# Gathering expert 3's rows earlier, and turning one row tile of expert 2 on TensorE, in an attention kernel followed by a hash-routed mixture of experts

## The chip, the cores and the metric

The kernel runs on one core of one Trainium2 chip. The metric is the device time of one execution in microseconds (us); lower is better. A core has TensorE (PE in the profile; its weight loads stand apart as PEld), VectorE (DVE), ScalarE (ACT), GpSimd (POOL) and SyncE (SP). 16 DMA engines move data between memory in HBM and the core's SBUF.

## The reference

The first half is attention over 8 batches, 12 heads, 448 positions and a head size of 64, with normalised q and k. Its output, as 3584 rows of 768 values, goes to the second half, in which each row is sent to one of 8 experts by a hash of its token id:

```
expert_idx = token_ids * 2654435761 % E          # E = 8
for e in range(E):
    mask = expert_idx == e
    xe = x[mask]                                  # about 448 rows of 768
    h = np.maximum(xe @ w1[e], 0.0)               # w1[e]: 768 x 1024
    out[mask] = h @ w2[e]                         # w2[e]: 1024 x 768
```

The change lies in the second half alone.

## The kernel before

**Attention** fills the first 160 us or so. It writes its rows, in fp16, to a scratch tensor in HBM (`x_scratch`), and a table of row numbers by expert (`gidx`) is worked out beside it.

**The experts** follow one after the other, e = 0 to 7. Each has 480 slots for its rows: three row tiles of 128 and one of 96 (`KT` = 4, `LAST` = 96). An expert goes through these steps.

- *Gather* (`fetch`, line 230): four indirect DMAs issued by POOL bring its rows from `x_scratch` into a ring of eight row tiles, `xg_ring` (the tile is called kr in the profile). Experts with an even number use tiles 0 to 3 of the ring, those with an odd number tiles 4 to 7.
- *Turn*: the rows must be turned, so that the 768 input values lie across the partitions, into `xT` (two buffers, used in turn by the experts). For experts 2 to 6 VectorE does it, in 16 instructions of 32 partitions each that take all four row tiles at a time (`turn_blocks`, line 1072). Experts 0 and 1 are turned by TensorE, six transposes for a row tile (`turn`, which calls `put_xT`: line 242, with a copy out of PSUM in line 244). Expert 7 is turned by four DMA transposes on SP.
- *First product* (`gemm1`, line 1002, 48 matmuls), whose result ScalarE evicts into `h_sb` (line 1011). It reads all of `xT` from its first matmul on.
- *Second product* (`gemm2`, line 1024, 16 matmuls for each of the four row tiles), evicted into `o_sb` (line 1034), from which POOL issues one indirect DMA for each row tile, the scatter, into the output (line 1037).

**Weights** come from HBM in five pieces an expert (three of w1, two of w2), each a DMA that POOL issues (`w_next`, line 1105) and that casts from fp32 to fp16. They are listed in `queue` and issued at fixed places in the program: two after an expert's first product, one behind each row tile of the second product, and what is left at the expert's end.

So POOL's program is one list of gathers, scatters and weight loads, all on one DMA queue. Each of these DMAs belongs to one of eight semaphores in turn, and the issue of a DMA waits for the one eight places before it, which had the same semaphore.

The order of work comes from the order in which the code is written (there is no scheduler). Two tables add work at given places: `plan[e, "k", kt]` lists functions that are called behind row tile kt of expert e's second product, and `before[e, kt]` functions that are called ahead of it. In the loop over the experts the places that the change touches are these:

```
            if e < E - 2:
                fetch(e + 2, range(KT))
                turn_blocks(e + 1)
            gemm1(...)
        if e:
            w_next(2)
```

Expert 2 is fetched in `plan[0, "k", 2]`, and expert 3 at the top of e = 1 by the lines above, behind the `w_next(len(queue))` that ends e = 0.

Of the kernel before, what the change touches and what calls it, by code (L numbers as in the profile page):

```python
# [20 lines left out]
def kernel(  # L21
# [30 lines left out]
    LAST = FIT - 3 * P  # L52
    KT = CAP // P
# [175 lines left out]
    def gather(xg, idx, rows=N):  # L229
        nc.gpsimd.indirect_dma_start(  # L230
            out=xg[0:idx.shape[0], :], out_offset=None, in_=x_dram[0:rows, :],
            in_offset=bass.IndirectOffsetOnAxis(ap=idx, axis=0),
            bounds_check=rows - 1, oob_is_err=False)
        return xg
# [729 lines left out]
    with tc.manual_schedule(), \  # L964
# [10 lines left out]
        def w1_view(e, w1_sb):  # L975
            return w1_sb[:].rearrange("p c (o f) -> p c o f" if e == 0 else "p c (f o) -> p c o f",
                                      o=FO)
# [13 lines left out]
        def gemm1(w1v, xT, h_sb, c0, c1, both=True, after=(), apart=0):  # L991
            banks = {}

            def products(fo, a0, a1):
                if fo not in banks:
                    banks[fo] = ps_h.tile([P, 512], FP32, name="h_ps")
                dst = banks[fo][:, a0 - c0:a1 - c0]
                if xT is xT_e:
                    dst = dst.rearrange("p (k t) -> p k t", t=P)
                for co in range(CO):  # L1000
                    src = xT[:, a0 // P:a1 // P, co, :] if xT is xT_e else xT[:, co, a0:a1]
                    nc.tensor.matmul(dst, lhsT=w1v[:, co, fo, :], rhs=src,  # L1002
                                     start=(co == 0), stop=(co == CO - 1))

            for fo in range(apart):
                products(fo, c0, c1 - P)
            for fo in range(FO):
                products(fo, c1 - P if fo < apart else c0, c1)
                h_ps = banks.pop(fo)
                if fo % 2 == 0 or not both:  # L1010
                    nc.scalar.activation(h_sb[:, fo, c0:c1], h_ps[:, :c1 - c0], AF.Relu)  # L1011
                else:
                    nc.vector.tensor_scalar(out=h_sb[:, fo, c0:c1], in0=h_ps[:, :c1 - c0],
                                            scalar1=0.0, scalar2=None, op0=ALU.max)
                for f in after[fo] if after else ():
                    f()

        def gemm2(w2_sb, h_sb, col, idx, free=True, between=None, last=False, by_v=True):
            w = LAST if free and col == KT - 1 else P
            o_ps = [ps_o.tile([P, DIN], FP32, name="o_ps")]  # L1020
            o_ps.append(ps_o.tile([P, DIN], FP32, name="o_ps") if last else o_ps[0])
            for d0, d1 in ((0, 512), (512, DIN)):
                for fo in range(FO):
                    nc.tensor.matmul(o_ps[d0 > 0][0:w, d0:d1], lhsT=h_sb[:, fo, col * P:col * P + w],  # L1024
                                     rhs=w2_sb[:, fo, d0:d1],
                                     start=(fo == 0), stop=(fo == FO - 1))
                if between and d0 == 0:
                    between()
                if last and d0 == 0:
                    o_sb = m_o.tile([P, DIN], FP32, name="o_sb")  # L1030
                    nc.scalar.copy(o_sb[0:w, 0:512], o_ps[0][0:w, 0:512])
            if not last:
                o_sb = m_o.tile([P, DIN], FP32, name="o_sb")
                (nc.vector.tensor_copy if by_v and col % 2 else nc.scalar.copy)(o_sb[0:w], o_ps[0][0:w])  # L1034
            else:
                nc.scalar.copy(o_sb[0:w, 512:DIN], o_ps[1][0:w, 512:DIN])
            scat = nc.gpsimd.indirect_dma_start(  # L1037
                out=out[:, :], out_offset=bass.IndirectOffsetOnAxis(ap=idx[0:w], axis=0),
                in_=o_sb[0:w], in_offset=None, bounds_check=N - 1, oob_is_err=False)
            if free:  # L1040

                tc.declare_no_dep(scat.ins, group="scatters", reason="disjoint rows")
                tc.add_to_no_dep_group("scatters", scat.ins)
# [4 lines left out]
        def fetch(e, kts):  # L1048
            for kt in kts:
                c = e * KT + kt  # L1050
                xgs[c] = gather(xg_ring[:, c % (2 * KT)],
                                gidx[0:P if kt < KT - 1 else LAST, c:c + 1],
                                N_EARLY if kt < KT - 1 else N)

        def turn(e, kt, copy=None):
            if e not in xTs:
                xTs[e] = m_x.tile([P, CO, CAP], FP16, name="xT")
            bank = ps_x.tile([P, DIN], FP16, name="xT_ps")
            put_xT(xgs.pop(e * KT + kt), xTs[e], kt, bank[:], copy)

        def turn_blocks(e):
            xT = xTs[e] = m_x.tile([P, CO, CAP], FP16, name="xT")
            c0 = e * KT % (2 * KT)
            xg = xg_ring[:, c0:c0 + KT].rearrange("p k (c m r) -> p k m c r", m=4, r=32)
            dst = xT[:].rearrange("p c (g r) -> p c g r", r=32)
            for kt in range(KT):
                xgs.pop(e * KT + kt)
            for i in range(4):
                n = KT if 32 * i < LAST else KT - 1
                g = slice(i, i + 4 * (n - 1) + 1, 4)  # L1070
                for m in range(4):
                    nc.vector.transpose(  # L1072
                        out=dst[32 * m:32 * m + 32, :, g].rearrange("p c k r -> p k c r"),
                        in_=xg[32 * i:32 * i + 32, 0:n, m])

        def turn_by_dma(e):
            xTs[e] = m_x.tile([P, CO, CAP], FP16, name="xT")
            for kt in range(KT):
                n = P if kt < KT - 1 else LAST
                nc.sync.dma_start_transpose(out=xTs[e][:, :, kt * P:kt * P + n],  # L1080
                                            in_=xgs.pop(e * KT + kt)[0:n, :])
# [20 lines left out]
        def w_next(n):  # L1102
            for _ in range(min(n, len(queue))):
                o, i = queue.pop(0)
                nc.gpsimd.dma_start(out=o, in_=i)  # L1105
# [135 lines left out]
        def each(f, *parts):  # L1241
            return [lambda p=p: f(p) for p in parts]
# [3 lines left out]
            (0, "g", 4): [p7, p8], (0, "g", 5): [p9, p10, p11],  # L1246
            (0, "g", 6): each(low, 0, 1), (0, "g", 7): each(low, 2, 3), (0, "k", 0): [high],
            (0, "k", 1): [high_tok], (0, "k", 2): [table_mm, lambda: fetch(2, range(KT))],
            (1, "k", 0): [overflow_table],
        }  # L1250
        t = lambda e, kt: (lambda: turn(e, kt))
        t0 = lambda e, kt: (lambda: turn(e, kt, nc.scalar.copy))
        before, between = {}, {}
# [2 lines left out]
        before[0, 2] = [lambda: gemm1_late(w1_view(0, w_tiles[0][0]), xTs.pop(0), hs[0], EARLY, FIT)]  # L1256
        between[0, 2] = t0(1, 2)
        before[0, 3] = [t(1, 3)]
        hs = {}
        fetch(0, [KT - 1])  # L1260
        fetch(1, [KT - 1])
# [2 lines left out]
        for e in range(E):  # L1264
            w1_sb, w2_sb = w_tiles[e]
            h_sb = hs[e] = m_h.tile([P, FO, CAP], FP16, name="h_sb")
            after = [plan.get((e, "g", fo), []) for fo in range(FO)]
            if e == 0:
                gemm1(w1_view(e, w1_sb), xTs[e], h_sb, 0, EARLY, False, after, 2)
            else:  # L1270
                if e == E - 2:
                    turn_by_dma(E - 1)
                if e < E - 2:
                    fetch(e + 2, range(KT))
                    turn_blocks(e + 1)
                gemm1(w1_view(e, w1_sb), xTs.pop(e), h_sb, 0, FIT, e >= E - 2, after)
            if e:
                w_next(2)
            if e == 2:
                n_ov = nc.values_load(novi[0:1, 0:1], min_val=0, max_val=NOV)  # L1280
            if e == E - 1:
                nc.gpsimd.drain()
            for kt in range(KT):
                c = e * KT + kt
                for f in before.get((e, kt), []):
                    f()
                gemm2(w2_sb, h_sb, kt, gidx[:, c:c + 1], between=between.get((e, kt)),
                      last=(c == E * KT - 1), by_v=e in (0, E - 2, E - 1))
                for f in plan.get((e, "k", kt), []):
                    f()  # L1290
                if e or kt > 1:
                    w_next(1)
            w_next(len(queue))
            if e + 4 < E:
                queue += w_pieces(e + 4)
# [47 lines left out]
```

## Time and profile before

| what | value |
|---|---|
| time, median of 3 runs | 333.07 us (332.08 to 333.38) |
| time of the profiled execution | 332.74 us |
| span of the profiled execution, first to last instruction | 331.1 us |
| TensorE busy (matmuls) | 318.2 us, 96% of the span |
| VectorE busy | 239.3 us, 72% |
| ScalarE busy | 207.5 us, 63% |
| GpSimd busy | 149.5 us, 45% |
| GpSimd's DMA queue (q0) | 58.32 MB; its packets took 87.7% of 16 engines' span |
| granted TensorE clock, mean | 0.994 |

A time is the device time of a whole execution; the span leaves out 1.6 us around the first and last instruction of the profiled one. TensorE is busy nearly all the time, but matmuls are pipelined and their ends are modelled, so that a row of matmuls can end after the next one starts. The start times are the ones to go by.

### The profile page before, as it was taken

To read this page: it belongs to the slowest core of one execution; us is meant where nothing else is said; L and a number is where in the kernel's file an instruction comes from. 1 tells how busy PE (TensorE), PEld (TensorE's weight loads), DVE (VectorE), ACT (ScalarE), POOL (GpSimd) and SP (SyncE) were. 2 spreads that over 40 slices of the span, in tenths; PEclk is the share of its full clock that TensorE was granted. 3 is DMA by queue.
4 is the path that set the end of the run, shared out by engine and by line. 5 is a ranking of instruction groups with operands and counts; after the bars stand their busy time and mean duration, and the time that the engine had idled before them with its cause. 6 is when DMAs were issued, how large, how long until landed. Compare 5 with 4: busy or idle time off the path is not lost. (4 is left out here: it accounts for less than half of the span.)

```text
span 331.1 us, 8985 instructions
## 1 busy us (share of the span) xinstructions
PE 318.2 (96%) x3765; PEld 219.7 (66%) x3765; DVE 239.3 (72%) x457; ACT 207.5 (63%) x317; POOL 149.5 (45%) x207
## 2 busy tenths in 40 slices
PE   7699999999999999999999999999999999999992
PEld 3467777777777777666767766666676675766761
DVE  4689999898999999985694397693958939422210
ACT  4699999999999999999543333424334253321211
POOL 8799944432441100003475872655727556403122
PEclk9999999999999999999999999999999999999997
DMA  6999999999999999722478699999999999993013
GB/s 122 197 202 203 194 242 196 236 200 240 203 240 212 245 225 227 164 70 70 124 152 211 165 207 242 244 264 265 265 272 239 254 253 260 307 174 137 23 48 124
DMA packets 45601, 65.52 MB, mean 198 GB/s; under 512 B 12727, under 2 KB 33423, under 8 KB 45432
## 3 DMA queue, kind: packets, MB, share of 16 engines
q0 software_dynamic: 39072, 58.32, 87.7%
q1 hardware_dynamic: 6328, 6.50, 7.5%
q8 instruction: 30, 0.49, 0.6%
q10 hardware_dynamic: 160, 0.11, 0.1%
q14 instruction: 11, 0.09, 0.1%
HBM read 89.29 MB, written 17.30 MB: 322 GB/s over the span
## 5 line engine op out<-in xcount | busy, mean ns | idle before, releaser
L660 ACT ACTIVATE expT<-sc_ps 128x896 bf16<-128x896 f32 x144 | 125.1, 960 | 1.0 <-PE sc_ps L637 0.7
L1072 DVE STREAM_TRANSPOSE xT<-kr 32x768 f16<-32x768 f16 (+1 forms) x80 | 73.6, 920 | 25.7 <-DMA kr<-x_scratch,gidx 15.2
L1024 PEld LDWEIGHTS <-h_sb 128*128 128x128 f16 (+1 forms) x512 | 52.2, 104 | 31.3
L1024 PE MATMUL o_ps<-w_sb,h_sb 128*128 128x512 f16 (+3 forms) x384 | 64.2, 326 | 0.0
L1011 ACT ACTIVATE h_sb<-h_ps 128x480 f16<-128x480 f32 (+1 forms) x56 | 31.3, 560 | 48.6 <-PE h_ps L1002 48.6
L1037 POOL DMA_INDIRECT out_dram<-o_sb,gidx x32 | 35.1, 1097 | 57.6 <-ACT o_sb L1034 29.6
L1034 ACT COPY o_sb<-o_ps 128x768 f32<-128x768 f32 (+1 forms) x26 | 20.8, 799 | 54.5 <-PE o_ps L1024 54.5
L230 POOL DMA_INDIRECT kr<-x_scratch,gidx x32 | 32.6, 1020 | 49.3 <-DVE qT L629 37.1
L1002 PEld LDWEIGHTS <-w_sb 128*128 128x128 f16 x300 | 39.8, 135 | 16.4 <-issue 0.7
L1002 PE MATMUL h_ps<-xT,w_sb 128*128 128x480 f16 x240 | 49.4, 366 | 0.3 <-DVE xT L1072 0.3
L637 PE MATMUL sc_ps<-qT,kT 64*128 64x448 f16 x288 | 44.4, 356 | 0.5 <-DVE qT L629 0.4
L678 PEld LDWEIGHTS <-expT 128*128 128x128 bf16 x846 | 36.8, 97 | 9.2 <-DVE x_sb L738 4.4
L678 PE MATMUL av_ps<-v,expT 128*128 128x65 bf16 x828 | 41.5, 193 | 0.1
L306 POOL DMA_DIRECT2D vr<-in_v_dram x36 | 23.7, 670 | 20.8 <-DMA kr<-in_k_dram 11.5
L738 DVE TENSOR_TENSOR x_sb<-av_ps,srec 128x448 f16<-128x448 f32 x47 | 29.3, 623 | 1.3
L663 ACT ACTIVATE expT<-sc_ps 128x448 bf16<-128x448 f32 x48 | 28.4, 595 | 0.1
L387 PEld LDWEIGHTS <-ident 128*128 128x128 f16 x576 | 22.6, 98 | 8.7 <-issue 4.4
L683 PE MATMUL av_ps<-v,expT 128*128 128x130 bf16 x138 | 24.0, 220 | 0.0
L1024 PE MATMUL o_ps<-kr,h_sb 128*128 128x512 f16 (+3 forms) x128 | 21.1, 326 | 0.0
L1002 PE MATMUL h_ps<-xT,qr 128*128 128x480 f16 x96 | 19.8, 366 | 0.5 <-DVE xT L1072 0.5
L637 PEld LDWEIGHTS <-kT 64*128 64x128 f16 x288 | 12.3, 93 | 9.5 <-issue 2.2
L1105 POOL DMA_DIRECT2D w_sb<-in_moe_w_dram x20 | 13.7, 692 | 9.4 <-DMA w_sb<-in_moe_w_dram 6.8
(226 smaller groups left out, 409.4 us busy)
## 6 DMA issues: line engine op xcount, KB each, us to landing
w_sb<-in_moe_w_dram POOLq DMA_DIRECT2D x18, 512.0 KB, 12.5
w_sb<-in_moe_w_dram POOLq DMA_DIRECT2D x8, 768.0 KB, 12.7
kr<-in_k_dram POOLq DMA_DIRECT2D x7, 672.0 KB, 15.6
qr<-in_q_dram POOLq DMA_DIRECT2D x7, 672.0 KB, 12.9
x_scratch<-x_sb SPq DMA_DIRECT2D x15, 288.0 KB, 6.4
w_sb<-in_moe_w_dram POOLq DMA_DIRECT2D x2, 1536.0 KB, 21.3
qr<-in_moe_w_dram POOLq DMA_DIRECT2D x6, 512.0 KB, 17.6
vr<-in_v_dram POOLq DMA_DIRECT2D x14, 192.0 KB, 13.6
```

Source lines behind the costliest of these rows:

```text
L230: nc.gpsimd.indirect_dma_start(out=xg[0:idx.shape[0], :], out_offset=None, in_=x_dram[0:rows, :], in_offset=bass.IndirectOffsetOnAxis(ap=i ...
L637: nc.tensor.matmul(sc[:, hh, :S], lhsT=kT[64 * hh:64 * hh + 64, P * j:P * j + P], rhs=qT[64 * hh:64 * hh + 64, :], start=True, stop=True)
L660: nc.scalar.activation(expT[:, 2 * j:2 * j + 2, :], sc[:, :, :S], AF.Exp, bias=0.0, scale=1.0)
L663: nc.scalar.activation(expT[:, 6, :], sc[:, 0, :S], AF.Exp, bias=0.0, scale=1.0)
L678: nc.tensor.matmul(av[:, 2 * t + hh, :], lhsT=expT[:, tl(hh, j), P * t:P * t + P], rhs=v8[:, i, vs(hh, j), 0:D + 1], start=(hh == 0 and t ...
L683: nc.tensor.matmul(av[:, 2 * t:2 * t + 2, :], lhsT=expT[:, 6, P * t:P * t + P], rhs=v8[:, i, 0::7, 0:D + 1], start=False, stop=False)
L738: nc.vector.tensor_tensor(out=xs[b][:, :, hp * D:hp * D + D], in0=av[:, :, :D], in1=srec[:, :, None].to_broadcast([P, SL, D]), op=ALU.mult)
L1002: nc.tensor.matmul(dst, lhsT=w1v[:, co, fo, :], rhs=src, start=(co == 0), stop=(co == CO - 1))
L1011: nc.scalar.activation(h_sb[:, fo, c0:c1], h_ps[:, :c1 - c0], AF.Relu)
L1024: nc.tensor.matmul(o_ps[d0 > 0][0:w, d0:d1], lhsT=h_sb[:, fo, col * P:col * P + w], rhs=w2_sb[:, fo, d0:d1], start=(fo == 0), stop=(fo == ...
L1037: scat = nc.gpsimd.indirect_dma_start(out=out[:, :], out_offset=bass.IndirectOffsetOnAxis(ap=idx[0:w], axis=0), in_=o_sb[0:w], in_offset=N ...
L1072: nc.vector.transpose(out=dst[32 * m:32 * m + 32, :, g].rearrange("p c k r -> p k c r"), in_=xg[32 * i:32 * i + 32, 0:n, m])
```

## The change

The four gathers of expert 3 are issued by POOL behind row tile 3 of expert 0's second product, ahead of the four weight loads of expert 3 that were issued there before, and no longer behind them. Of expert 2's rows, tiles 0 to 2 are turned by VectorE as before, in 16 instructions of three tiles each; tile 3 (96 rows) is turned by six TensorE transposes ahead of row tile 2 of expert 1's second product, and copied out of PSUM by ScalarE.

```diff
-        def turn_blocks(e):
+        def turn_blocks(e, tiles=KT):
...
-            for kt in range(KT):
+            for kt in range(tiles):
                 xgs.pop(e * KT + kt)
             for i in range(4):
-                n = KT if 32 * i < LAST else KT - 1
+                n = tiles if 32 * i < LAST else min(tiles, KT - 1)
...
             (0, "k", 1): [high_tok], (0, "k", 2): [table_mm, lambda: fetch(2, range(KT))],
+            (0, "k", 3): [lambda: fetch(3, range(KT))],
...
         before[0, 3] = [t(1, 3)]
+        before[1, 2] = [t0(2, KT - 1)]
...
                 if e < E - 2:
-                    fetch(e + 2, range(KT))
-                    turn_blocks(e + 1)
+                    if e > 1:
+                        fetch(e + 2, range(KT))
+                    turn_blocks(e + 1, KT if e > 1 else KT - 1)
```

`t0(e, kt)` is a call of `turn` with ScalarE's copy. At e = 0 the third line from the end has nothing left to fetch, since expert 2 was fetched in `plan`.

POOL, from the end of expert 0 to the beginning of expert 1. L1105 is a weight load (the first ones for expert 3, the last pair for expert 4), L230 a gather (of expert 3's four row tiles into the ring, kr_69), L1037 a scatter.

```order
 L1105 DMA w_sb<-in_moe_w_dram 128x2x1024
 L1037 DMA out_dram<-o_sb,gidx 3584x768
+L230 DMA kr_69<-x_scratch,gidx 128x768 x3
+L230 DMA kr_69<-x_scratch,gidx 96x768
 L1105 DMA w_sb<-in_moe_w_dram 128x2x1024 x2
 L1105 DMA w_sb<-in_moe_w_dram 128x3072 x2
-L230 DMA kr_69<-x_scratch,gidx 128x768 x3
-L230 DMA kr_69<-x_scratch,gidx 96x768
 L1105 DMA w_sb<-in_moe_w_dram 128x2x1024 x2
 L1037 DMA out_dram<-o_sb,gidx 3584x768
```

The four gathers moved ahead of four loads; no DMA is added or taken away, and from the two loads that follow on the order is the same.

VectorE, from the last eviction of expert 0 to the beginning of expert 3's turn. The first group of L1072 turns expert 2, the second expert 3; DMASW and a number is one of the eight semaphores of POOL's DMAs.

```order
 L1034 COPY o_sb<-o_ps 96x768 [waits PE_49]
-L1072 STREAM_TRANSPOSE xT<-kr_69 32x4x6x32 [waits DMASW5_49,DMASW6_49,DMASW4_49,DMASW3_49]
-L1072 STREAM_TRANSPOSE xT<-kr_69 32x4x6x32 x11
-L1072 STREAM_TRANSPOSE xT<-kr_69 32x3x6x32 x4
+L1072 STREAM_TRANSPOSE xT<-kr_69 32x3x6x32 [waits DMASW5_49,DMASW4_49,DMASW3_49]
+L1072 STREAM_TRANSPOSE xT<-kr_69 32x3x6x32 x15
 L1234 TENSOR_TENSOR ovc<-iota_f,oend 128x256
 L1237 TENSOR_REDUCE ovf<-ovc 128x32 [waits DVE_49]
 L1238 TENSOR_SCALAR ov_i<-ovf 128x32 [waits DVE_49]
-L1072 STREAM_TRANSPOSE xT<-kr_69 32x4x6x32 [waits DMASW5_49,DMASW6_49,DMASW0_49,DMASW7_49,PE_49,Activation_49]
+L1072 STREAM_TRANSPOSE xT<-kr_69 32x4x6x32 [waits DMASW2_49,DMASW3_49,DMASW1_49,DMASW4_49,PE_49,Activation_49]
```

Twelve instructions of four tiles became instructions of three, and expert 2's turn waits for three gathers and no longer for four.

TensorE, in expert 1's second product, between its row tiles 1 and 2. L242 is a transpose, of which there are six pairs.

```order
 L1024 LDWEIGHTS h_sb
 L1024 MATMUL o_ps<-w_sb,h_sb 128x256
+L242 LDWEIGHTS kr_69
+L242 MATMUL xT_ps<-ident_75,kr_69 128x96
...
 L1024 LDWEIGHTS h_sb
 L1024 MATMUL o_ps<-w_sb,h_sb 128x512
```

Six transposes stand there that did not before; nothing else on TensorE moved.

## Rows read from the trace of the kernel before

**Rows 1.** The page, 40 slices of the span (8.28 us each): DMA engines' busy tenths.

```profile
DMA  6999999999999999722478699999999999993013
```

**Rows 2.** Timeline of PE, 182 to 331 us: start, length, engine, line, instructions, idle before.

```profile
192.66 10.56 PE L1024 MATMUL o_ps<-w_sb,h_sb 128*128 128x512 f16 x64
203.75 9.88 PE L1002 MATMUL h_ps<-xT,qr 128*128 128x480 f16 x48 [0.52 <-DVE xT L1072]
213.46 10.56 PE L1024 MATMUL o_ps<-kr,h_sb 128*128 128x512 f16 x64
224.37 9.88 PE L1002 MATMUL h_ps<-xT,w_sb 128*128 128x480 f16 x48 [0.34 <-DVE xT L1072]
234.09 10.56 PE L1024 MATMUL o_ps<-w_sb,h_sb 128*128 128x512 f16 x64
244.55 9.88 PE L1002 MATMUL h_ps<-xT,w_sb 128*128 128x480 f16 x48
...
294.58 10.56 PE L1024 MATMUL o_ps<-kr,h_sb 128*128 128x512 f16 x64
304.98 9.88 PE L1002 MATMUL h_ps<-xT,w_sb 128*128 128x480 f16 x48
```

**Rows 3.** Timeline of DVE, 168 to 275 us (columns as in rows 2).

```profile
188.78 14.92 DVE L1072 STREAM_TRANSPOSE xT<-kr 32x768 f16<-32x768 f16 x16 [4.68 <-DMA kr<-x_scratch,gidx]
...
204.64 0.47 DVE L1238 TENSOR_SCALAR ov_i<-ovf 128x32 int32<-128x32 f32 x1
209.41 14.91 DVE L1072 STREAM_TRANSPOSE xT<-kr 32x768 f16<-32x768 f16 x16 [4.30 <-ACT h_sb L1011]
229.58 14.92 DVE L1072 STREAM_TRANSPOSE xT<-kr 32x768 f16<-32x768 f16 x16 [5.26 <-DMA kr<-x_scratch,gidx]
```

**Rows 4.** Timeline of POOL, 168 to 275 us (columns as in rows 2).

```profile
181.92 1.05 POOL L230 DMA_INDIRECT kr<-x_scratch,gidx  x1 [0.30 <-issue]
...
185.88 0.96 POOL L230 DMA_INDIRECT kr<-x_scratch,gidx  x1 [0.30 <-PE h_ps L1002]
186.85 0.81 POOL L1105 DMA_DIRECT2D w_sb<-in_moe_w_dram  x1
187.97 0.99 POOL L1037 DMA_INDIRECT out_dram<-o_sb,gidx  x1 [0.30 <-issue]
188.94 2.63 POOL L1105 DMA_DIRECT2D w_sb<-in_moe_w_dram  x4
191.87 1.08 POOL L230 DMA_INDIRECT kr<-x_scratch,gidx  x1 [0.30 <-issue]
...
195.88 0.99 POOL L230 DMA_INDIRECT kr<-x_scratch,gidx  x1 [0.30 <-issue]
...
214.77 1.06 POOL L230 DMA_INDIRECT kr<-x_scratch,gidx  x1 [1.38 <-DMA w_sb<-in_moe_w_dram]
```

**Rows 5.** Issue to landing: gathers of 181 to 187, of 191 to 197; scatter of 187.97.

```profile
DMA to landing us min/median/max: 2.8/3.1/3.1
...
DMA to landing us min/median/max: 13.3/15.1/15.9
...
out_dram<-o_sb,gidx POOLq DMA_INDIRECT x1, 6.2
```

**Rows 6.** Windows: stretch, length, POOL busy, PE clock, DMA engines' share, GB/s.

```profile
184.00:186.00 2.00, 1.39 (x3) 1.00 0.53 171
...
190.00:192.00 2.00, 1.70 (x4) 1.00 1.10 196
```

**Rows 7.** Timeline of PE, 170 to 260 us: transposes of a 96-row tile (columns as in rows 2).

```profile
180.09 0.42 PE L242 MATMUL xT_ps<-ident,kr 96*128 96x96 f16 x6
180.34 2.77 PE L1024 MATMUL o_ps<-w_sb,h_sb 128*96 128x512 f16 x16
```

**Rows 8.** Groups by line and shape, DVE, 188 to 204 us: busy us, mean ns.

```profile
L1072 DVE STREAM_TRANSPOSE xT<-kr 32x768 f16<-32x768 f16 x12 | 11.6, 969 | 4.8 <-DMA kr<-x_scratch,gidx 4.7
L1072 DVE STREAM_TRANSPOSE xT<-kr 32x576 f16<-32x576 f16 x4 | 3.1, 772 | 0.1
```

## The prediction

> **What bounds the kernel now.** I read the timeline of TensorE first. From 160 us to the end its matmuls follow each other without a gap, except at two places: expert 2's first product starts at 203.75 after 0.52 us of idle time, expert 3's at 224.37 after 0.34 us, both released by VectorE's turn [rows 2]. Because ends of matmuls are modelled, starts tell the loss better. From the start of a second product to the start of the next first product is 304.98 - 294.58 = 10.40 us where nothing holds it (expert 7, which VectorE does not turn). For expert 2 it is 203.75 - 192.66 = 11.09, for expert 3 224.37 - 213.46 = 10.91, for expert 4 244.55 - 234.09 = 10.46 [rows 2]. So 0.69, 0.51 and 0.06 us are lost there. A first product takes 213.46 - 203.75 = 9.71 us. That makes 20.11 us for an expert that waits for nothing.
>
> Next, VectorE's timeline. A turn takes 14.92 us: 188.78 to 203.70 for expert 2, 209.41 to 224.32 for expert 3, 229.58 to 244.50 for expert 4 [rows 3]. Each ends 0.05 us before TensorE starts the product that reads it [rows 2, 3]. The reader should see that this holds for expert 4 too, where TensorE shows no idle time. That turn is as late as TensorE can bear, so anything that brings TensorE there sooner makes it wait. Experts 5 and 6 repeat expert 4.
>
> What holds the turns is the arrival of the rows. Expert 4's turn was released by its gathers [rows 3]. Expert 3's row names ScalarE as the releaser, but its last gather was issued at 195.88 and the shortest landing of that group is 13.3 us, so it came in at 209.2 [rows 4, 5]. VectorE was free from 205.11 on [rows 3].
>
> Last, the DMA queue. Gathers of expert 2, on a quiet queue, landed 2.8 to 3.1 us after their issue; those of expert 3, issued behind a scatter and five weight loads, after 13.3 to 15.9 us [rows 4, 5]. The DMA engines are at 0.53 of their time while expert 2's gathers go out, and at 1.10 by 190 us [rows 6], and stay full to about 295 us [rows 1]. In that stretch the bytes set when rows arrive, not POOL: expert 4's first gather at 214.77 waited for a weight load to land [rows 4]. So TensorE and the DMA queue run side by side at nearly the same pace, 20.11 us against 229.58 - 209.41 = 20.17 us for an expert [rows 2, 3].
>
> **The change part by part.** *Turning expert 2.* VectorE now has 16 instructions of three tiles: 16 x 772 ns = 12.4 us at most [rows 8]. It waits for three gathers and not the fourth, so it can start about 1.3 us sooner than 188.78 (the spacing of the gathers is (185.88 - 181.92) / 3 = 1.32 us [rows 4]), near 187.5, and ends by 200. Nothing in it is needed before 203. The wait of 0.69 us goes. TensorE pays for six transposes of a 96-row tile: 180.34 - 180.09 = 0.25 us from their start to that of the next matmul [rows 7]. The tile has long landed at that point (185.88 + 3.1 = 189.0 [rows 4, 5], against 192.66 plus two row tiles, about 197.9). ScalarE's copy is at nothing: it stands between evictions of row tiles that come every 2.6 us (10.40 / 4) on an engine busy 63% overall, and if it took a whole microsecond it would still end 4 us before the product at 203.3. If that cover were gone, its length would fall on that product. Expert 2's product then starts at 192.66 + 10.40 + 0.25 = 203.31, which is 0.44 us sooner.
>
> *Turning expert 3.* POOL reaches the gathers at 187.97 + 0.99 + 0.30 = 189.26 and issues them to about 194.5, at the old spacing. They land by 197 (unqueued 196.3, with some queueing behind the scatter, which landed at 187.97 + 6.2 = 194.17 [rows 4, 5]). VectorE is free from about 201.4 (200 and its three small instructions), so the turn runs from there to about 216.3, 7 us ahead of need. The 0.51 us goes: expert 3's first product would start at 203.31 + 9.71 + 10.40 = 223.42, 0.95 us sooner than before.
>
> *What is late next.* TensorE would then want expert 4's `xT` at 223.42 + 9.72 + 10.40 = 243.54. That turn cannot begin before expert 4's rows are in. Those gathers stand behind the same DMAs as before: four gathers and four loads have changed places, and all of it is ahead of them. So the turn ends at 244.50 + D, where D is what the new order costs or gives the queue by then. The whole 0.95 us is given back as one wait in front of expert 4's first product, and from there on the program runs D later. The loads that are now behind the gathers are not missed: they are weights that are read from 223 on, and with a gather's worth of delay (below) they land by about 209.
>
> *The size of D.* The trace does not have the new order. Lower bound: the queue is full from 189 us on in the old order, and the bytes are the same, so it cannot be ahead of before; 0. Upper bound: while expert 2's gathers went out alone the engines were at 0.53 against 1.10 for a full queue [rows 6], so half of the 4 x 1.32 us that the four issues take would be lost, 2.7 us. But there is cover that those had not: a load issued at 186.85 and a scatter that landed at 194.17 [rows 4, 5] keep the engines busy while three of the four gathers are written. What is left is from there to the first load behind the gathers, issued at about 194.5 and started some 2 us later (estimated from a gather's unqueued 2.8 us less its own transfer, 0.53 x 1.32 = 0.7): 2.3 us. In it lie four gathers' transfers of 0.6 us each (in the old order four moved in about 2.3 us: the first landed at 191.87 + 15.9 = 207.8, the last at 209.2, and a gather's own time comes before the first [rows 4, 5]). Work and time nearly match, so the engine that finishes last, which decides a landing, hardly runs dry, the quicker ones for some tenths. I take D = 0.3, far nearer the covered case than the bare one, since the scatter's landing is a row of that very place.
>
> *A rule that speaks against it.* Expert 3's gathers are issued under VectorE's turn in either order. Before, they went out at 191.87 to 195.88, 1.34 us apart, with VectorE busy turning; expert 2's, with VectorE mostly free, 1.32 us apart [rows 3, 4]. The Trainium skill ("SBUF — State Buffer", section "Who interferes with whom") says that GpSimd can't write DMA descriptors while VectorE holds the port they share. By that rule each of the four could wait for a turn instruction of 0.8 us, and D would be some 3 us larger. The rows show no such wait for this instruction, and the sum goes by them.
>
> **The sum.** 332.74 us (the profiled execution, 331.1 of span and 1.6 around it) - 0.44 - 0.51 + 0.95 + 0.3 = 333.0 us; the 0.06 us that expert 4 lost before is in the 0.95. The median of the runs shown lies 0.33 us above that execution, so the time to expect is 333.3 us.
>
> **The rivals.** *The gain is kept.* If expert 4's rows came about 1 us sooner, the 0.95 us would stay and the time be 333.07 - 0.95 = 332.1 us. For it: the DMA engines do four gathers while they would wait less. Against it: the queue is full in both orders, and expert 4's gathers wait for the same load to land. Chance 0.10. Even this is less than what a measurement of this kernel can tell from no change, about 0.5% or 1.7 us.
>
> *The queue runs dry.* The gathers are issued one by one, 1.32 us apart, where loads are issued four in 2.63 us [rows 4]. If the cover ends early or the first load starts late, D comes near 2.7 us. The time is then 333.07 + 2.7 = 335.8 us at the worst, 334.5 at half of it, and the kernel is slower by 0.5% from D = 1.7 on. All of it would appear as a wait before expert 4's first product (0.95 + D). For it: the 0.53. Against it: the scatter landing at 194.17. Chance 0.17 for D over 1, about half of it over 1.7.
>
> *VectorE's hold on the descriptors*, the rule above: 333.07 + 3 = 336 us. Against it the 1.34 us. Chance 0.02.
>
> *The change doesn't do what it says*: the transposes or ScalarE's copy make expert 2 wait as long as before. That costs up to 0.7 us at 203 but is inside the 0.95 us that expert 4 gives back, so the time stays 333.3. It is part of the forecast's cases.
>
> **How the numbers follow.** The forecast (D from 0 to 1, no gain kept) has 0.71, its own range being 332.5 to 334.3 with the spread of the runs. To leave out no more than 2 in 10 the range takes in most of the kept gain and half of the dry queue: 331.9 to 334.8. Faster by over 0.5% needs more than TensorE lost at these places in all (0.69 + 0.51 + 0.06): 0.04. Slower by over 0.5%: half of the dry queue and the hold on descriptors, 0.10. The rest, 0.86, is within 0.5%.
>
> **What would show it.** In the profile after, expert 2's and 3's first products start near 203.3 and 223.4 with no idle time before them; expert 2's turn has 16 instructions of 576 columns; expert 3's gathers land within some 4 us of their issue; and there is a new wait of about 1 us before expert 4's first product, released by VectorE, whose turn starts when its gathers land near 229.9. If expert 4's product starts at 243.6, the step "same bytes ahead, same arrival" is wrong. If it starts after 246, the size of D is. Experts 5 to 7 should keep their 20.1 to 20.2 us; if they do not, the queue did not carry D along.

## The result and the profile after

The changed kernel took 336.15 us (median of 13 runs, 333.67 to 337.79) against 332.79 us of the kernel before (13 runs, 331.54 to 334.97), a ratio of 1.0085 with a 95% interval of 1.0062 to 1.0108. It is slower by about 2.8 us, outside the range that was given. In a second comparison the ratio was 1.0100 (1.0064 to 1.0137). Among all the kernels below, one execution (337.97 us, gathers behind two loads) counts as slow and is left out of its ratio.

The profiled execution is the quickest of the 13, 333.67 us with a span of 332.1 us. Its attention happened to end sooner: expert 1's second product starts at 191.04, against 192.66 in [rows 2], although nothing ahead of it was changed but one place in POOL's list. To compare the two, count from that start. The timeline of TensorE (start, length, engine, line, instructions, idle before):

```profile
191.04 5.36 PE L1024 MATMUL o_ps<-w_sb,h_sb 128*128 128x512 f16 x32
196.24 0.42 PE L242 MATMUL xT_ps<-ident,kr 96*128 96x96 f16 x6
196.50 5.37 PE L1024 MATMUL o_ps<-w_sb,h_sb 128*128 128x512 f16 x32
201.70 9.88 PE L1002 MATMUL h_ps<-xT,qr 128*128 128x480 f16 x48
211.42 10.56 PE L1024 MATMUL o_ps<-kr,h_sb 128*128 128x512 f16 x64
221.82 3.81 PE L1002 MATMUL h_ps<-xT,w_sb 128*128 128x480 f16 x18
225.81 6.24 PE L1002 MATMUL h_ps<-xT,w_sb 128*128 128x480 f16 x30 [0.19 <-ACT h_sb L1011]
231.89 10.56 PE L1024 MATMUL o_ps<-w_sb,h_sb 128*128 128x512 f16 x64
245.59 9.88 PE L1002 MATMUL h_ps<-xT,w_sb 128*128 128x480 f16 x48 [3.14 <-DVE xT L1072]
```

Expert 2's first product starts 10.66 us after expert 1's second product began (11.09 before), and expert 3's 10.40 us after expert 2's (10.91 before): both waits are gone, and the six transposes cost 0.26 us. In front of expert 4 there is a new one. From 231.89 to 245.59 are 13.70 us where 10.40 are needed, so TensorE waits 3.30 us. Counted from the start above, expert 4's product comes at 54.55 us against 51.89: 2.66 us later. VectorE's timeline says why:

```profile
186.18 12.52 DVE L1072 STREAM_TRANSPOSE xT<-kr 32x576 f16<-32x576 f16 x16 [3.71 <-DMA kr<-x_scratch,gidx]
199.92 14.91 DVE L1072 STREAM_TRANSPOSE xT<-kr 32x768 f16<-32x768 f16 x16
230.63 14.91 DVE L1072 STREAM_TRANSPOSE xT<-kr 32x768 f16<-32x768 f16 x16 [15.79 <-DMA kr<-x_scratch,gidx]
```

Expert 3's turn now starts as soon as VectorE is free and ends at 214.83, 7 us ahead of need. Expert 4's waited 15.79 us for its rows, and began 39.59 us after expert 1's second product, against 36.92 in [rows 3]. The prediction's D is therefore 2.67 us, where 0.3 was forecast. The queue shows part of it. Windows of POOL (stretch, length, POOL busy, PE clock, DMA engines' share, GB/s):

```profile
188.00:190.00 2.00, 1.70 (x2) 1.00 1.08 188
190.00:192.00 2.00, 1.39 (x3) 1.00 0.93 323
192.00:194.00 2.00, 2.00 (x3) 1.00 0.57 171
194.00:196.00 2.00, 2.00 (x5) 1.00 0.93 118
196.00:198.00 2.00, 1.70 (x2) 1.00 1.09 197
```

In the old order the share was 1.09 over this stretch:

```profile
190.00:200.00 10.00, 6.60 (x9) 1.00 1.09 207
```

Here it falls to 0.57 while expert 3's gathers are served: (0.16 + 0.52 + 0.16) / 1.09 x 2 us = 1.5 us of all engines are lost. The share hides a little more: from 194 to 196 us the engines are busy at 0.93 but move 118 GB/s, against 197 in the next window, so that the loads behind the gathers start slowly. That is (1 - 118 / 197) x 2 = 0.8 us, of which the share has 0.3. POOL's timeline has the gathers at 187.65 to 191.61, 1.32 us apart as before, then six loads in one row; expert 4's first gather is the last line:

```profile
187.65 1.04 POOL L230 DMA_INDIRECT kr<-x_scratch,gidx  x1 [0.30 <-issue]
...
191.61 0.98 POOL L230 DMA_INDIRECT kr<-x_scratch,gidx  x1 [0.30 <-issue]
192.59 4.09 POOL L1105 DMA_DIRECT2D w_sb<-in_moe_w_dram  x6
...
215.95 1.06 POOL L230 DMA_INDIRECT kr<-x_scratch,gidx  x1 [2.79 <-DMA w_sb<-in_moe_w_dram]
```

Expert 4's first gather is issued 24.91 us after expert 1's second product began, against 214.77 - 192.66 = 22.11 in [rows 4], and in both kernels it waited for a weight load to land. So the lateness is in the queue before expert 4's gathers are issued.

Expert 3's gathers landed quickly, 3.3 to 5.7 us after their issue (13.3 to 15.9 in [rows 5]):

```profile
DMA to landing us min/median/max: 3.3/4.7/5.7
```

That short landing is the same fact as the low share: there was little ahead of them in the queue.

### The profile page after: what moved, and what is told of

It is laid out like the page before. It is cut to its first block, busy times and chain, and to the rows that moved or that the text cites. A ratio compares the mean times of both kernels' runs of the same rounds, so it can differ in the third digit from the quotient of the medians.

```text
span 332.1 us, 8998 instructions
## 1 busy us (share of the span) xinstructions
PE 317.9 (96%) x3771; PEld 220.1 (66%) x3771; DVE 236.7 (71%) x457; ACT 207.6 (62%) x318; POOL 148.3 (45%) x207
## 5 line engine op out<-in xcount | busy, mean ns | idle before, releaser
L1072 DVE STREAM_TRANSPOSE xT<-kr 32x768 f16<-32x768 f16 (+1 forms) x80 | 71.2, 890 | 30.8 <-DMA kr<-x_scratch,gidx 24.5
L1037 POOL DMA_INDIRECT out_dram<-o_sb,gidx x32 | 35.1, 1096 | 60.6 <-ACT o_sb L1034 26.9
L230 POOL DMA_INDIRECT kr<-x_scratch,gidx x32 | 32.6, 1017 | 50.4 <-DVE qT L629 37.0
L640 PE MATMUL sc_ps<-qT,kT 128*128 128x448 f16 x48 | 16.9, 353 | 0.4 <-ACT expT L660 0.4
```

Of the source, the lines that this page charges most:

```text
L230: nc.gpsimd.indirect_dma_start(out=xg[0:idx.shape[0], :], out_offset=None, in_=x_dram[0:rows, :], in_offset=bass.IndirectOffsetOnAxis(ap=i ...
L1037: scat = nc.gpsimd.indirect_dma_start(out=out[:, :], out_offset=bass.IndirectOffsetOnAxis(ap=idx[0:w], axis=0), in_=o_sb[0:w], in_offset=N ...
L1072: nc.vector.transpose(out=dst[32 * m:32 * m + 32, :, g].rearrange("p c k r -> p k c r"), in_=xg[32 * i:32 * i + 32, 0:n, m])
```

## The experiments

For each kernel, three numbers are read from the timelines: how late expert 4's turn starts counted from expert 1's second product, less the 36.92 us of before (D); TensorE's wait before expert 4's first product (start to start, less 10.40 us); and the ratio to the kernel before, run on the same chip. The last column is the number of executions with a mean granted clock of 0.992 or less; of the kernel before it was 12 of the 87 executions beside these runs. The kernels are explained one by one below.

| kernel | D, us | wait, us | ratio, 95% interval | low clock |
|---|---|---|---|---|
| the change | 2.67 | 3.30 | 1.0085 (1.0062 to 1.0108) | 9 of 13 |
| the change again | 4.38 | 3.21 | 1.0100 (1.0064 to 1.0137) | 5 of 6 |
| gathers alone moved | 2.12 | 2.62 | 1.0073 (1.0051 to 1.0095) | 6 of 12 |
| last tile alone turned by TensorE | 0.51 | 0.45 | 1.0020 (0.9994 to 1.0045) | 2 of 12 |
| gathers behind two loads | 0.27 | 1.25 | 1.0000 (0.9974 to 1.0026) | 2 of 12 |
| gathers behind one load | 1.53 | 2.52 | 1.0065 (1.0036 to 1.0095) | 1 of 8 |
| wait filled with matmuls | 3.04 | 3.20 | 1.0054 (1.0026 to 1.0081) | 1 of 12 |
| before, expert 4's rows late | 2.63 | 2.90 | 1.0079 (1.0055 to 1.0104) | 7 of 12 |
| the change, later rows ahead | -2.14 | 0 | 0.9959 (0.9938 to 0.9979) | 3 of 12 |
| behind two loads, later rows ahead | -3.94 | 0 | 0.9956 (0.9936 to 0.9977) | 0 of 7 |
| the change, row of loads broken | 2.85 | 3.22 | 1.0104 (1.0068 to 1.0140) | 6 of 6 |
| behind one load, row of loads broken | 1.65 | 2.64 | 1.0086 (1.0057 to 1.0116) | 5 of 10 |

**The change once more.** No edit.

> The changed kernel once more, for a second profile. Theory 1 (the queue ran dry while expert 3's gathers were issued one by one): every DMA behind them lands 2 to 3 us later, counted from the start of expert 1, and TensorE waits about 3 us before expert 4's first product (3.14 us in the first profile); the time is 2 to 3 us over before. Theory 2, on top of it (that wait lets the granted clock fall in some executions): this execution shows a mean clock under 0.993, a stretch behind the wait with a lower granted clock, and a time over 335.5 us. Rival (the spread from 333.7 to 337.8 us comes from attention): the products after 182 us are as in the first profile, and the difference lies ahead of them.

This profile has the highest time of its six runs, 339.2 us, with a clock of 0.998. The wait before expert 4 is there again, and two more:

```profile
229.75 6.24 PE L1002 MATMUL h_ps<-xT,w_sb 128*128 128x480 f16 x30 [1.77 <-ACT h_sb L1011]
...
249.43 9.88 PE L1002 MATMUL h_ps<-xT,w_sb 128*128 128x480 f16 x48 [3.05 <-DVE xT L1072]
...
271.20 9.88 PE L1002 MATMUL h_ps<-xT,w_sb 128*128 128x480 f16 x48 [1.49 <-DVE xT L1072]
```

So the spread does not come from attention alone: D itself varies, here 4.38 us, and it was paid again at expert 5. Theory 2's forecast for this execution failed (its clock did not fall). The other five have mean clocks of 0.988 to 0.992 and times over 336.5 us, as theory 2 has it, but no profile of them shows where the clock fell.

**One half of the change at a time.** First the gathers alone:

```diff
-        before[1, 2] = [t0(2, KT - 1)]
...
-                    turn_blocks(e + 1, KT if e > 1 else KT - 1)
+                    turn_blocks(e + 1, KT)
```

> Only the gathers of expert 3 are moved; VectorE turns all four row tiles of expert 2, as before. Theory 1: the whole loss is the queue's, so it is as slow as the changed kernel, 2 to 3 us over before, with about 0.5 us of wait before expert 2 and about 2.7 us before expert 4. Rival (the transposes and ScalarE's copy in expert 1's second product cost the time): the same as before or up to 0.5 us faster.

Then the turn alone:

```diff
-            (0, "k", 3): [lambda: fetch(3, range(KT))],
...
-                    if e > 1:
-                        fetch(e + 2, range(KT))
+                    fetch(e + 2, range(KT))
```

> Only the last row tile of expert 2 is turned by TensorE; the gathers of expert 3 stay behind the four loads. Theory 1: no DMA changes its place, so the queue stays full; the wait before expert 2 goes, the one before expert 3 grows to about 0.8 us, and the time is that of before within 0.5 us. Rival (the transposes cost the time): 1 us or more over before.

Ratios of 1.0073 and 1.0020: the loss belongs to the moved gathers, not to the transposes or ScalarE's copy. In the second kernel expert 2 starts without a wait and expert 3 waits 0.90 us in place of 0.34, as expected: one half of the change only hands the wait on to the next expert. The profile of the first shows what the long wait can do to the clock. Windows of TensorE (stretch, length, PE busy, granted clock, DMA share, GB/s), around expert 4's first product, which starts at 247.10 after 2.46 us without work:

```profile
244.00:247.10 3.10, 0.64 (x6) 1.00 1.04 234
248.00:249.00 1.00, 1.00 (x4) 0.50 1.04 335
249.00:250.00 1.00, 1.00 (x4) 0.50 1.05 334
250.00:251.00 1.00, 1.00 (x4) 0.50 1.12 234
252.00:253.00 1.00, 1.00 (x6) 1.00 1.15 227
```

The clock is granted at half, the lower of its two levels (1.2 GHz of 2.4), for about 3.5 us. The product takes 11.40 us from its start to that of the next (247.10 to 258.50) and not 9.71: 1.69 us on top of the wait. The Trainium skill ("TensorE: Matmul & The Clock Gate", section "HAM oscillation — how this bites in real kernels") describes such a fall after a wait for data. The trace agrees here with 2.46 us of idle time, but in the first profile 3.14 us of it left the clock at 1.00.

**The wait filled.** The changed kernel with matmuls on TensorE, whose results nobody reads, ahead of expert 4's first product:

```diff
+                if e == 4:
+                    keep_busy(w_tiles[3][1], 15)
```

> The changed kernel with 15 more matmuls of 384 columns (about 2.4 us, results unused) on TensorE ahead of expert 4's first product, where it waits about 3.1 us. Theory 2 (that wait lets the granted clock fall to half for about 4 us in most executions, which costs some 1.7 us): the clock stays at 0.994 or more in nearly all executions, and the median is 1 to 1.7 us under the changed kernel's 337 of the last comparison, 1.5 to 2.5 us over before. Rival (the executions with a low mean clock lose it elsewhere, or the low clock costs nothing): clocks and median as in the changed kernel, or later by the added matmuls.

The profile has the added matmuls (line 1079) where most of the idle time was:

```profile
244.26 2.60 PE L1079 MATMUL xT_ps<-w_sb 128*128 128x384 f16 x15
247.46 9.88 PE L1002 MATMUL h_ps<-xT,w_sb 128*128 128x480 f16 x48 [0.60 <-DVE xT L1072]
```

Low clocks went from 14 of 19 executions to 1 of 12, and the ratio from 1.0085 and 1.0100 to 1.0054, while D (3.04) and the wait, start to start, stayed. The next kernel, run on the same chip with its wait not filled, had 7 low clocks of 12. The work that TensorE gets there is useless, and yet the ratio is lower with it. The difference of the ratios, 0.3 to 0.5% or 1 to 1.5 us, is the clock's part by these runs; their intervals overlap, so the count of low clocks is the firmer evidence. A mean clock does not say where the clock fell: one profile further down (the change with later rows ahead, mean 0.991) has its fall at 10 to 16 us, within attention, and no wait before expert 4. It is the count against the 12 of 87 of the kernel before that ties most of the falls to the wait.

**The rows late, nothing else.** The kernel before, with one weight load of 512 KB issued ahead of expert 4's gathers and no longer behind them:

```diff
+                    if e == 2:
+                        w_next(1)
                     fetch(e + 2, range(KT))
...
-                w_next(2)
+                w_next(1 if e == 2 else 2)
```

> The kernel before, with one thing moved: expert 4's gathers are issued behind one weight load of 512 KB more. Nothing is issued one by one into a quiet queue. Theory 1 (whatever delays expert 4's rows is paid in full by TensorE, since their turn ends as TensorE wants it): the rows come 2.5 us later, TensorE waits 2.4 to 2.6 us before expert 4's first product, and the time is 2.5 us over before, with theory 2 up to 4 us in executions whose clock falls (mean clock 0.992 or less). Rival (expert 4 has slack, and the loss of the changed kernel comes from the queue's state and not from these rows): within 0.7 us of before.

D is 2.63 us with a full queue (a share of 1.10 from 190 to 200 us), the wait 2.90 us, and the ratio 1.0079:

```profile
247.50 9.88 PE L1002 MATMUL h_ps<-xT,w_sb 128*128 128x480 f16 x48 [2.74 <-DVE xT L1072]
```

The runs fall into two groups: five with clocks of 0.995 to 0.997 at 335.28 to 335.92 us, seven with 0.990 to 0.992 at 336.90 to 338.17. Late rows of expert 4 alone thus make nearly the whole result, clock included.

**The gathers behind loads.** Expert 3's gathers behind two of the four loads:

```diff
-            (0, "k", 3): [lambda: fetch(3, range(KT))],
...
+            if e == 0:
+                w_next(1)
+                fetch(3, range(KT))
             w_next(len(queue))
```

> As the changed kernel, but expert 3's gathers are issued behind two of the four loads instead of ahead of all. Theory 1: the two loads (about 5 us of transfers) cover the gathers' single issues, the queue stays full, gathers of expert 3 land by 203 and their turn ends by 218, ahead of need; expert 4's rows come as before, with a wait of about 0.95 us before its first product; time that of before within 0.6 us. Rival (any gather ahead of loads delays what follows, covered or not, because the bytes are in another order): 2 us or more over before, with a wait of about 3 us before expert 4.

And behind one:

```diff
             if e == 0:
-                w_next(1)
                 fetch(3, range(KT))
```

> The changed kernel with expert 3's gathers behind one of the four loads (none in the changed kernel, two in the one that kept the queue full). Theory 1: one load of 512 KB is 2.5 us of transfers, as much as the queue lacked (1.5 us by the engines' share of 0.93 against 1.09 over 10 us), so the share from 190 to 200 us is back over 1.05, the wait before expert 4's first product is 1 to 1.5 us and the time within 0.8 us of before. Rival (any step of the gathers ahead of loads costs in proportion, half of the changed kernel's loss for half of the way): 1.2 to 1.8 us over before with a wait of about 2 us.

Behind two loads the share from 190 to 200 us is full, D is 0.27 us, the wait 1.25 and the time that of before (1.0000). A window of TensorE and its timeline:

```profile
190.00:200.00 10.00, 10.00 (x62) 1.00 1.07 225
...
245.26 9.88 PE L1002 MATMUL h_ps<-xT,w_sb 128*128 128x480 f16 x48 [1.09 <-DVE xT L1072]
```

This is what the prediction forecast for the change itself. Behind one load the expectation failed. The share is nearly full too, yet D is 1.53 us and the ratio 1.0065:

```profile
190.00:200.00 10.00, 10.00 (x65) 1.00 1.06 230
```

So the idle queue is not all of D. In both this kernel and the changed one there is a stretch, some 20 us into expert 1's second product, in which the engines are busy and move little. In the changed kernel, windows of POOL:

```profile
208.00:210.00 2.00, 0.54 (x1) 1.00 1.13 212
210.00:212.00 2.00, 0.00 (x0) 1.00 1.06 155
```

The engines move 155 GB/s there and not 212, which costs (1 - 155 / 212) x 2 = 0.5 us. The kernel before has 214 and 219 GB/s at that place, the one with two loads ahead 210 and 216. With one load ahead it is 197 and 146, which costs 0.8 us in the same way.

**The row of loads broken.** What the kernels with that stretch had in common was five or six loads issued in a row. In two more kernels, the change and the one with one load ahead, the first two loads of expert 4 stand behind expert 1's first scatter:

```diff
-            if e:
+            if e > 1:
                 w_next(2)
...
-                    w_next(1)
+                    w_next(3 if (e, kt) == (1, 0) else 1)
```

> The changed kernel with expert 4's first two weight loads issued behind the first scatter of expert 1 and no longer in one row of six loads. What is open is why the rows come 2.7 us late when the engines' share accounts for 1.5 us of an idle queue. If the row of six loads makes a stretch of slow transfers (about 20 us into expert 1's second product, some 0.5 us of all engines, seen in each kernel with six loads in a row), it goes: expert 4's rows come 0.4 to 0.7 us sooner by start of expert 1, the wait shrinks from 3.1 to about 2.5 us. Rival (the stretch has to do with something else): wait and time as in the changed kernel, 1.0085 to 1.01 of before.

> The same for the kernel with expert 3's gathers behind one load. There the engines' share from 190 to 200 us was already 1.06, and yet expert 4 waited 2.36 us. If the row of loads slows transfers, the wait falls to 1.3 to 1.8 us and the time to within 0.8 us of before. Rival (the gathers' place alone sets it): a wait of 2.2 to 2.5 us, and 1.2 us or more over before.

The rival held. D was 2.85 and 1.65 us, the waits 3.22 and 2.64, the ratios 1.0104 (1.0068 to 1.0140) and 1.0086 (1.0057 to 1.0116). The slow stretch is still there (181 GB/s at a share of 0.90 from 210 to 212 us in the first). The row of loads alone does not make it; what does stays open.

**Expert 4's rows taken out of the path.** The changed kernel, with the gathers of experts 4 to 7 issued earlier:

```diff
-                    if e > 1:
-                        fetch(e + 2, range(KT))
...
+                if kt == 1 and 0 < e < E - 3:
+                    fetch(e + 3, range(KT))
```

> The changed kernel, and the gathers of experts 4 to 7 are issued behind row tile 1 of the second product three experts before (two weight loads and two scatters sooner). The queue still runs dry while expert 3's gathers are issued. Theory 1 (the dry queue costs time only because expert 4's rows stand behind it): those rows come some 6 to 9 us sooner, the wait before expert 4 goes, no first product of experts 2 to 6 waits, the clock stays at 0.994 or more, and the time is 0.5 to 1.2 us under before. Rival (a queue that is 2 us late is paid further along, by evictions that wait for scatters or by weights that come late): 1 us or more over before, with new waits of TensorE.

This one answered another question. Behind row tile 1 of expert 1 the gathers of expert 4 stand ahead of TensorE's transposes of expert 2's last tile, which lie in the same ring tile. TensorE waited 23.74 us there for rows of expert 4, turned them in place of expert 2's, and so did not compute the reference. The time was 359.08 us; the kernel with the same edit and the gathers behind two loads, of which 0.8 to 1.3 us under before was expected, did the same and took 356.12 us. The edit was then made with `kt == 2`, behind those transposes:

> The changed kernel, and the gathers of experts 4 to 7 are issued behind row tile 2 of the second product three experts before, one weight load and one scatter (about 4.6 us of transfers) sooner, and behind TensorE's transposes of expert 2's last tile. The queue still runs dry while expert 3's gathers are issued. Theory 1 (the dry queue costs time only because expert 4's rows stand behind it): the rows come 4 to 5 us sooner than in the changed kernel, the wait of 3.1 us before expert 4 goes or shrinks under 0.3 us, the clock stays at 0.994 or more in most executions, and the time is 0.5 to 1.3 us under before. Rival (a queue that is 2 us late is paid further along, by evictions that wait for scatters or by weights): 1 us or more over before, with new waits of TensorE of that size.

> As the last one, but expert 3's gathers stand behind two of the four loads, so that the queue does not run dry either. Both theories: no first product of experts 2 to 6 waits over 0.2 us, and the time is 0.8 to 1.3 us under before. If the dry queue costs nothing but expert 4's rows it equals the last one within 0.5 us; if it is paid elsewhere too it is 1 us or more faster than it.

The ratios are 0.9959 and 0.9956, 331.15 and 330.84 us against 332.60. Both are a little further under before than was forecast, by 1.4 and 1.5 us. The first still has the dry queue (0.93 from 190 to 200 us), and yet no product waits for its rows. So the wait of 3 us came from expert 4's rows. The late queue is not free elsewhere: in the first kernel's profile the first products of experts 4 to 6 stop after 18 matmuls for 0.24, 0.16 and 0.34 us, and take 0.41, 0.34 and 0.51 us longer than 9.71 from start to start. That is 1.26 us in all, part of what the rival had forecast. The first of the three:

```profile
247.33 6.24 PE L1002 MATMUL h_ps<-xT,w_sb 128*128 128x480 f16 x30 [0.24 <-ACT h_sb L1011]
```

This is ScalarE, which waited 3.75 us for a scatter to land before it could reuse an `o_sb` buffer. In the second kernel all of them come 20.12 us apart:

```profile
222.14 9.88 PE L1002 MATMUL h_ps<-xT,w_sb 128*128 128x480 f16 x48
231.86 10.56 PE L1024 MATMUL o_ps<-w_sb,h_sb 128*128 128x512 f16 x64
242.26 9.88 PE L1002 MATMUL h_ps<-xT,w_sb 128*128 128x480 f16 x48
251.98 10.56 PE L1024 MATMUL o_ps<-w_sb,h_sb 128*128 128x512 f16 x64
262.38 9.88 PE L1002 MATMUL h_ps<-xT,w_sb 128*128 128x480 f16 x48
```

From expert 1's second product to expert 7's first are 302.62 - 191.36 = 111.26 us here, against 304.98 - 192.66 = 112.32 before and 112.49 in the first kernel. So only the second kernel's profile shows the gain in the experts; the times of the two kernels do not tell them apart. The second beats the kernel before by 0.44% and the changed one by about 1.3%. The kernel before with nothing but the gathers of experts 4 to 7 moved was not run, so how much of the 0.44% is owed to the change and how much to that edit is not shown. The profile alone speaks for a part of the change: the waits before experts 2 and 3, 1.20 us in [rows 2], are gone for 0.26 us of transposes.

## Why the prediction was wrong

**What held.** The bound was read rightly: TensorE and the DMA queue side by side, with VectorE's turn of expert 4 as late as TensorE can bear. Expert 2's wait went for 0.26 us of transposes (0.25 forecast). Expert 3's turn ended 7 us early (7 forecast). Experts 5 to 7 kept their pace in the first profile; in the second, expert 5 waited once more. The step that all of the gain is handed to expert 4 and paid back there held too: with the queue kept full (gathers behind two loads) the change is worth nothing.

**What failed is the size of D.** The sum had 0.3 us; it is 2.67 us in the first profile, 2.1 to 4.4 us in the kernels that issue the gathers ahead of all four loads and leave those of expert 4 in their place. Counted from the start that the prediction used, expert 4's product starts at 245.59 + 1.62 = 247.2, past the 246 that was named as the sign of a wrong D. An upper bound of 2.7 us was in the text, with the dry queue as its mechanism and 335.8 us as its price, but as a rival: a D over 1 had a chance of 0.17. The reason for choosing 0.3 was that a load and a scatter would cover the gathers' single issues and that the last engine would hardly run dry. Three things were wrong in it.

- The gap behind the cover was not filled. The scatter landed 5.4 us after its issue, at 191.8, when three gathers had been issued and the fourth was being written, 0.8 us sooner than forecast if counted from the first gather. The sum then left four whole gathers, 2.4 us of transfers, for the 2.3 us up to the first load. But part of them had moved under the cover: from 190 to 192 us the engines moved 323 GB/s x 2 us = 0.65 MB, twice the 0.30 MB of the whole scatter (96 rows of 3,072 B). What was left filled half of the engines' time, a share of 0.57 from 192 to 194 us. The engines do run dry, by 1.5 us, and the loads behind them start slowly, 0.5 us more. The kernel with two loads as cover shows D nearly gone.
- Transfers are slower by about 0.5 us for a stretch some 20 us later. The prediction had no term for this, and its cause is not known. With one load of cover it is 0.8 us, about half of a D of 1.53 us. In the first profile these three terms (1.5, 0.5 and 0.5 us) come to 2.5 of the 2.67 us.
- The bound of 2.7 us was itself too low, since it had the idle time alone, and D changes from one execution to the next: 2.67 and 4.38 us in two profiles of the same kernel. In the second, the same three terms give about 2.6 us, and POOL issued expert 4's four gathers over 5.28 us in place of 4.17, because it waited between them for a scatter and a load to land. What makes up the rest, and why the two executions differ, is not known. A single profile of before could not show that spread.

**What was missing is the clock.** The prediction priced a wait of TensorE at its length and put nothing for the clock behind it. In the profile of the gathers alone moved, the clock fell to half behind the wait and cost 1.69 us more. The times agree: 336.22 us is the median of the changed kernel's nine executions with low clocks, 334.54 us that of the four others, just inside the range's upper end of 334.8 us. Filling the wait took most of the low clocks away. The clock is not the whole miss, though: with the wait filled the ratio is still 1.0054, and the slowest execution of the second comparison, 339.2 us, had a clock of 0.998 and lost its time in waits.

**The rule on VectorE and GpSimd** made no difference that shows: the gathers were issued 1.32 us apart under the turn, as before.

**A wait that was not foreseen** is the 0.19 us at 225.81 in expert 3's first product (1.77 us in the second profile). It comes from ScalarE, whose copy of the last row tile came late. In the second profile that copy had waited 4.09 us for a scatter to land, since `o_sb` has five buffers; the scatters are as late as everything else in the queue. It cost nothing in the end, because expert 4 waited anyway.

## What to carry to other kernels

When a transfer is moved ahead in a full queue, ask what covers its issue: the four gathers here went out 1.3 us apart and left the engines at about half of their time, and all that stood behind them was late. A wait that is removed where the next stage has no slack is only handed on, so look for the edit that gives slack to the last in the line, here the gathers of all later experts. And a wait of TensorE of some 3 us should be priced with the chance of a slower clock behind it.

## What the runs showed of the hardware

The clock's fall after a wait is not certain. Over the kernels whose wait before expert 4 was 2.5 to 3.3 us and was not filled, 39 of 67 executions had the low mean clock, from 1 of 8 (gathers behind one load) to 6 of 6 (the change with its loads broken up), against 12 of 87 of the kernel before. Of their seven profiles two show a fall at this place, with 2.46 and 3.05 us of idle time before expert 4's first product (1.69 and 1.40 us longer in that product). Five show none, with 2.36 to 3.14 us, one of them with 3.05 us as well. So the length of the wait alone does not decide it; what does was not found.

The stretch in which transfers are slow (146 to 181 GB/s in a window of 2 us, for 0.5 to 0.8 us) appeared in all eight profiles of kernels that gather expert 3's rows ahead of three or four loads and compute the reference, and in none of those with these gathers behind two loads or four. It is not clear in the kernel that turned the wrong rows, with these gathers ahead of four loads (201 GB/s or more). Breaking up the loads that follow did not remove it.
